# GpSimd's weight sums cut into small pieces and moved in front of the pair sums; two token sums moved behind the last pair's additions

## The chip, the cores and the metric

The kernel runs on one core of one Trainium2 chip. The metric is the device time of one execution in microseconds (us), the median of several runs. Before the change it is 717.16 us (three runs, 717.06 to 717.26).

## The reference

One transformer block over 2048 tokens of width 1024, in bfloat16: a linear attention with 32 heads behind a layer norm, and a gated feed-forward network of inner width 3584.

```python
def reference(A_x, A_wqkv, A_wo, B_x, B_W_gate, B_W_up, B_W_down):
    def _A_ref(x, wqkv, wo):
        ...
        phi = lambda t: jnp.where(t > 0, t + 1, jnp.exp(t)) + 1e-6
        pq, pk = phi(q), phi(k)
        kv = jnp.einsum("bhsd,bhse->bhde", pk, v)
        z = jnp.einsum("bhsd->bhd", pk)
        num = jnp.einsum("bhqd,bhde->bhqe", pq, kv)
        den = jnp.einsum("bhqd,bhd->bhq", pq, z)[..., None] + 1e-6
        o = num / den
        return ... @ wo
    def _B_ref(x, W_gate, W_up, W_down):
        ...
        h = gate * up
        return jnp.einsum("bsf,fd->bsd", h, W_down)
    x = A_x
    h = x + _A_ref(_layernorm(x, axis=-1), A_wqkv, A_wo)
    h2 = h + _B_ref(_layernorm(h, axis=-1), B_W_gate, B_W_up, B_W_down)
    return h2
```

## The kernel before

Nearly all matrix products go by Strassen's scheme with seven products in place of eight (P1 to P7), which needs sums of blocks of the weights and of the tokens beforehand, and additions of the partial results afterwards. TensorE (PE) runs the products; VectorE (DVE), ScalarE (ACT) and GpSimd (POOL) make the sums, the copies between PSUM banks ("forks": a bank's partial sum is copied into a second bank, and both are then accumulated further) and the additions.

The order of work is written out by hand. The program is one list of operations for each engine; every engine runs its own list strictly in order, and an operation waits on semaphores for what it reads and for the last users of what it overwrites. DMAs are issued almost all from SyncE's list (SP), in order as well. A list of hooks says between which products of PE the other engines' operations are put into their lists.

The change lies in the stage of the output projection `@ wo` (about 169 to 226 us of the span) and at its seam with the feed-forward stage. The stage has two parts:

- **Ten direct tiles**, d = 0 to 9, of 128 tokens each: `a4_mm(d)` issues 16 plain matmuls of 512 columns into a pair of banks; between them, at places that the table `at` names, `nd` issues the attention quotient of a later tile: `a2_num` (32 small matmuls on PE, into banks 0 to 3) and `a2_div` (three operations on DVE, L1320, L1323, L1325, and the transposing DMA "T3d" on SP, L641, which fills `oT`). So `nd` at tile d makes the token tile d + 4. For d up to 7, `a4_h(d)` adds the residual (DVE, L1465) into one of three slots of `hsb`, stores that row block by DMA, and makes the statistics of the second layer norm: `mean` and `square` on ACT (L885), each followed by small one-column operations on POOL (L891, L906, L909, and "lnn", L1481). `a4_norm(d - 1)` then normalises the tile before (ACT, L1491) and, up to tile 3, issues its transposing DMA "T5d" into `hnT`; those of 4 to 7 are issued later. Tiles 8 and 9 have their residual put into the banks beforehand by ACT (`a4_pre`, "hx") and are read out by ACT.
- **Three pairs of tiles by Strassen**, `o_group(p0)`, `o_group(p0 + 1)`, `o_group(p0 + 2)`, for the tiles 10/11, 12/13, 14/15. The products come in the order P1, P7, P6, P2, P5, P4, P3, four matmuls each. P7, P6, P5 and P3 read the pair sums So3, So2, So1, So4 (`o_sums`, POOL, L1383); P7, P6, P5 and P4 read weight sums TWo3, TWo2, TWo1, TWo4 (`wo_sums`, POOL, L1366). P6 goes into a bank that the fork "ofk1" (ACT, L850) fills from P1's bank, and P5 into one that "ofk2" fills from P6's. The additions `fin` (DVE, L1422) leave the residual stream of the pair in `hp_home`: tile 11 in the slot of `hsb` that held tile 8. The last addition of a pair and its store wait in `o_pend` until hook 1 of the next.

POOL has three more duties in this stage. TWo3 and TWo1 are made during the query products before it, in eight pieces of 128x512. TWo2 and TWo4 are made behind the tiles 2 to 5, in four pieces of 128x1024 (`tw`). And the weight sums T1 to T4 of the feed-forward stage's first unit (`pool_t`, L1572, eight pieces of 128x512) are spread from tile 6 to the end of the last pair. DVE makes the token sums S1 to S4 of the feed-forward stage (`ss`, L1548, 128x2048 each) in hooks 1, 3, 5 and 7 of the last pair; they need the `hnT` of tiles 0 to 7.

The feed-forward stage begins with unit 0: P1 for two halves (banks 1 and 0), each followed by a fork "fk1" (ACT, L850, into banks 4 and 5), one product P5 with S1, then P2 into banks 1 and 0, and so on; S2, S3 and S4 are read later in the unit, by P6, P7 and P3. On DVE it begins with four sums "xs" (L1628) and three "g1" (L1606).

Of the kernel before, what the change touches and what calls it, by code (L numbers as in the profile page):

```python
# [6 lines left out]
ALU = mybir.AluOpType  # L7
# [125 lines left out]
def bass_sequential_preLN__linear_attn_block__glu_gated_reglu__prompt_kernel(  # L133
# [34 lines left out]
    KH = NDC // 2  # L168
# [8 lines left out]
    TPP = TOK // P  # L177
# [27 lines left out]
    with es:  # L205
# [9 lines left out]
        NXN = 4  # L215
# [76 lines left out]
        xo = RA[:, 12 * D:16 * D].rearrange("p (a b) -> p a b", a=NXN)  # L292
# [79 lines left out]
        s2 = sb("s2", [P, 2, 5], f32)  # L372
# [7 lines left out]
        def bank(b, w=512):  # L380
            return ps[:, b, 0:w]
# [40 lines left out]
        B_bank = bufs("bank", 8)  # L422
# [521 lines left out]
        def run(ops, n):  # L944
            for _ in range(min(n, len(ops))):
                ops.pop(0)()
# [410 lines left out]
        def wo_sums(j, eng, k0, k1, deps=()):  # L1357
            def w(k, h):
                return wo[:, k * KH + k0:k * KH + k1, h * NW:(h + 1) * NW], [B_wo[h]]

            def t(i):
                return TWo(i)[:, k0:k1, :], [B_TWo[i]]

            x, y = {2: lambda: (w(1, 1), w(0, 1)), 0: lambda: (w(0, 1), w(0, 0)), 1: lambda: (w(1, 1), t(0)),
                    3: lambda: (w(1, 0), t(1))}[j]()
            PL.add(eng, lambda e: e.tensor_tensor(out=t(j)[0], in0=x[0], in1=y[0], op=ALU.subtract),  # L1366
                   reads=x[1] + y[1], writes=[B_TWo[j]], deps=deps, name="TWo%d" % (j + 1))
# [15 lines left out]
            PL.add(eng, lambda e: e.tensor_tensor(out=s(i)[0], in0=x[0], in1=y[0], op=op), reads=x[1] + y[1],  # L1383
                   writes=[B_So[z][i]], name="So%d_%d" % (i + 1, p))

        def o_group(p, bks, hooks, fin_eng):
            sa, sb2 = 2 * p, 2 * p + 1
            z = p % 2
            a, f, b, c = bks
            s7, sc, fx = (btmp[:, 1, :], B_bt[1]), (btmp[:, 0, :], B_bt[0]), (Ef[:, z, :], B_Ef[z])  # L1390

            def X(k, t):
                st = 2 * p + t
                return (lambda kk: oT(st)[:, k * KH + kk, :]), [B_oT[st % NOT]]

            def SX(i):
                return (lambda kk: So[:, z, i, kk, :]), [B_So[z][i]]

# [12 lines left out]
            def hook(i):  # L1411
                for f_ in o_pend.pop(i, ()):
                    f_()
                for f_ in hooks.get(i, ()):
                    f_()

            def half(st, h):
                return hp_home[st][:, h * NW:(h + 1) * NW], B_hp[st][h]

            def fin(d, bk, o, nm, eng="dve"):  # L1420
                i = [bank(bk), [B_bank[bk]]] if isinstance(bk, int) else bk
                PL.add(eng, lambda e: e.tensor_tensor(out=d[0], in0=i[0], in1=o[0], op=ALU.add), reads=i[1] + o[1],  # L1422
                       writes=[d[1]], name=nm)
# [24 lines left out]
            fin(half(sb2, 1), [sc[0], [sc[1]]], (fx[0], [fx[1]]), "hp_%d_1" % sb2, fin_eng)  # L1448
            hook(5)
            prod(b, X(1, 1), TW(3), False, "P4")  # L1450
            fin(half(sb2, 0), b, (s7[0], [s7[1]]), "h_%d_0" % sb2)
            store(sb2)
            hook(6)
            prod(c, SX(3), W(1, 1), False, "P3")
            o_pend[1] = [lambda: fin(half(sa, 1), c, res(sa, 1), "h_%d_1" % sa), lambda: store(sa)]
            hook(7)

        o_pend = {}

        def a4_h(st):  # L1460
            xs = x2_slot(st)
            hs = st % NHS
            b = a4_bank.pop(st)
            if st < TPP:
                PL.add("dve", lambda e: e.tensor_tensor(out=hsb[:, hs, :], in0=ps[:, b:b + 2, :],  # L1465
                                                        in1=x2(st).rearrange("p (a c) -> p a c", a=2), op=ALU.add),
                       reads=[B_bank[b], B_bank[b + 1], B_x2[xs]], writes=[B_hs[hs]], name="h_%d" % st)
            dma(sl_hs[hs], ov[st * P:(st + 1) * P, :], hsb[:, hs, :], "st_h_%d" % st, reads=[B_hs[hs]],
                writes=[B_hscr[st]])
            if st + 2 < NDIR:  # L1470
                a4_pre(st + 2)
# [5 lines left out]
            for f_ in act_stats(src, [B_hs[hs]], xo[:, st % NXN, :], B_xo[st % NXN], s2[:, ks, 0:4], B_s2[ks],  # L1477
                                "ln2_%d" % st):
                f_()
            m_, r_, n_ = s2[:, ks, 0:1], s2[:, ks, 2:3], s2[:, ks, 4:5]  # L1480
            PL.add("pool", lambda e: e.tensor_scalar(out=n_, in0=m_, scalar1=r_, scalar2=-1.0, op0=ALU.mult,  # L1481
                                                     op1=ALU.mult),
                   reads=[B_s2[ks][0], B_s2[ks][2]], writes=[B_s2[ks][4]], name="lnn_%d" % st)
# [940 lines left out]
        def sums(p, *what):  # L2424
            return [lambda i=i, e=e: o_sums(p, i, e) for i, e in what]

        def tw(j, k0):
            return lambda: wo_sums(j, "pool", k0, k0 + 2)

        def t5(st):  # L2430
            return lambda: a4_t(st)

        def ldx(st):
            return lambda: load_x2(st)

        def pt():
            run(pool_t, 1)

        p0 = NDIR // 2
        at = {0: {15: [nd]}, 1: {14: [nd]}, 2: {13: [nd]}, 3: {11: [nd]}, 4: {9: [nd]}, 5: {7: [nd]},  # L2440
              6: {5: [nd]}, 7: {3: [nd]}, 8: {1: [nd, t5(4)], 14: [nd, ldx(13), ldx(12)]}, 9: {11: [nd]}}
        aft = {2: [tw(1, 0)], 3: [tw(1, 2)], 4: [tw(3, 0)], 5: [tw(3, 2)], 6: [pt, pt],
               7: sums(p0, (2, "pool"), (0, "pool")), 8: sums(p0, (1, "pool"), (3, "pool")) + [pt]}
        H_PAIRS.sort(key=lambda b: max(bank_last[b], bank_last[b + 1]))
        for d in range(2):
            a4_pre(d)
        for d in range(NDIR):
            a4_mm(d, at.get(d, {}))
            a4_h(d)
            run(late_phi, 1)  # L2450
            if 1 <= d <= TPP:
                a4_norm(d - 1)
            if d < 2:
                load_w_next()
            for f_ in aft.get(d, ()):
                f_()
        o_group(p0, [4, 6, 5, 7], {
            1: [nd, t5(5), t5(6)], 6: [t5(7), ldx(15), ldx(14)],
            4: sums(p0 + 1, (2, "pool"), (0, "pool"), (1, "pool"), (3, "pool"))}, "dve")
        load_w_next()  # L2460
        o_group(p0 + 1, [4, 2, 5, 7], {
            2: sums(p0 + 2, (2, "pool"), (0, "pool"), (1, "pool"), (3, "pool")), 6: [pt]}, "dve")
        load_w_next()
        o_group(p0 + 2, [4, 6, 5, 7], {1: [pt, ss[0]], 2: [pt], 3: [ss[1]], 5: [ss[2]], 7: [ss[3]]}, "dve")
        for f_ in o_pend.pop(1):
            f_()
        run(pool_t, len(pool_t))
        for q in range(NWR):
            load_wraw(q)
        load_w_next()  # L2470
# [179 lines left out]
```

## Time and profile before

| | |
|---|---|
| median of the runs | 717.16 us (717.06 to 717.26) |
| profiled execution, its own time | 717.18 us |
| its span, first to last instruction | 715.5 us |
| PE busy | 703.6 us, 98% of the span |
| DVE busy | 608.7 us, 85% |
| ACT busy | 413.1 us, 58% |
| POOL busy | 144.1 us, 20% |
| granted TensorE clock | 1.00 throughout |

All times below are microseconds from the start of the span. In the timeline view a line has the start, the duration, the engine, the source line, the operation, the tiles written and read, the shape and how many were merged; in square brackets stand the engine's idle time before it and what ended that. A matmul of 512 columns is shown as 0.38 long, but the next one starts 0.216 later (a product of four starts 0.86 after the product before it), so the time that PE really lost at a wait is the distance between the starts less that cadence, some 0.16 more than the idle time shown.

### The profile page before, as it was taken

The numbers are of one execution on the slowest core, as the hardware profiler recorded it, in microseconds if no ns is written. First come the engines' busy times: TensorE is split into PE (matmuls) and PEld (weight loads), VectorE is DVE, ScalarE is ACT, GpSimd is POOL, SyncE is SP. The second block draws the span as 40 slices with busy tenths as digits, with TensorE's granted clock in tenths as the row PEclk, the third lists the DMA queues.
The fourth block names the chain that finished last, engine by engine and source line by source line (L and its number), as shares of the span: only waits on it lengthen the run. The fifth ranks groups of instructions, "written<-read, shape, count | busy, mean of one in ns | idle before, by whom it ended". The sixth has DMA issues, their size and how long they took to land.

```text
span 715.5 us, 13215 instructions
## 1 busy us (share of the span) xinstructions
PE 703.6 (98%) x4984; PEld 392.9 (55%) x5039; DVE 608.7 (85%) x974; ACT 413.1 (58%) x744; POOL 144.1 (20%) x202
## 2 busy tenths in 40 slices
PE   9999999999999999999999999999999999999998
PEld 4444444444443445454544558865555555547887
DVE  7988867899868899999998787788889888988985
ACT  4887666764963777887786401036666667633010
POOL 3321100111797213132312002310000000000331
PEclk9999999999999999999999999999999999999999
DMA  9753345015997899999897999995343534267997
GB/s 301 258 98 81 38 131 165 23 31 97 208 219 203 272 342 296 322 251 294 264 312 225 267 249 318 316 234 161 90 132 112 155 107 131 80 206 250 324 317 186
DMA packets 195104, 144.21 MB, mean 202 GB/s; under 512 B 53984, under 2 KB 172512, under 8 KB 195040
## 3 DMA queue, kind: packets, MB, share of 16 engines
q1 hardware_dynamic: 190048, 138.77, 67.1%
q0 software_dynamic: 4032, 3.67, 3.5%
q8 instruction: 40, 0.66, 0.4%
q10 hardware_dynamic: 960, 0.92, 0.4%
q14 instruction: 24, 0.20, 0.1%
HBM read 98.76 MB, written 32.51 MB: 183 GB/s over the span
## 4 chain that ended last, share of the span: by engine, by line
PE 91%; DVE 5%; issue 2%; ACT 1%; DMA 1%; DVEq 0%; ACTq 0%
PE ps L845 91%; DVE RC L1548 1%; DMA RAB<-RXH 1%; DVE RO L1572 1%; DVE RAB L1422 0%; DVE RAB L1706 0%; ACT RXH L885 0%; DMA RE<-in_A_x_dram 0%; DVE RW L781 0%; ACT ps L850 0%; ACT RX L850 0%; DVE RWG L1093 0%; PE ps L1006 0%; DVE ps L1706 0%; DVE RE L1967 0%
## 5 line engine op out<-in xcount | busy, mean ns | idle before, releaser
L850 ACT ACTIVATE ps<-ps 128x512 f32<-128x512 f32 (+1 forms) x263 | 133.1, 517 | 180.4 <-PE ps L845 127.6
L845 PE MATMUL ps<-RC,RO 128*128 128x512 f16 x616 | 147.0, 369 | 0.0
L845 PEld LDWEIGHTS ps<-RC,RO 128*128 128x128 f16 x616 | 60.1, 98 | 53.1 <-ACT ps L850 1.2
L850 ACT ACTIVATE RE<-ps 128x512 f32<-128x512 f32 (+3 forms) x106 | 63.8, 627 | 31.7 <-PE ps L845 17.6
L845 PE MATMUL ps<-RC,RWG 128*128 128x512 f16 x320 | 80.8, 379 | 0.0
L845 PE MATMUL ps<-RH,RWG 128*128 128x512 bf16 (+1 forms) x347 | 77.6, 348 | 1.4 <-ACT ps L850 1.4
L1976 POOL DMA_DIRECT2D out_dram<-RX x20 | 17.9, 1258 | 271.5 <-DVE RX L1967 218.4
L845 PE MATMUL ps<-RH,RO 128*128 128x512 bf16 (+1 forms) x228 | 59.2, 379 | 1.5
L1706 DVE TENSOR_TENSOR RE<-ps,RE 128x1024 bf16<-128x1024 f32 (+1 forms) x42 | 44.0, 1047 | 18.2 <-PE ps L845 18.1
L845 PE MATMUL ps<-RW,RAB 128*128 128x256 f16 (+3 forms) x370 | 55.6, 303 | 0.2
L845 PEld LDWEIGHTS ps<-RH,RWG 128*128 128x128 bf16 x348 | 33.9, 98 | 36.9 <-ACT ps L850 2.0
L845 PE MATMUL ps<-RAB 128*128 128x512 bf16 (+3 forms) x248 | 52.6, 349 | 1.1 <-ACT ps L850 0.8
L845 PEld LDWEIGHTS ps<-RC,RWG 128*128 128x128 bf16 (+1 forms) x320 | 30.0, 98 | 34.4 <-ACT ps L850 5.8
L845 PEld LDWEIGHTS ps<-RW,RAB 128*128 128x128 f16 (+1 forms) x374 | 36.3, 98 | 16.2 <-ACT RX L850 1.1
L1967 DVE TENSOR_TENSOR RE<-ps,RE 128x512 f32<-128x512 f32 x44 | 30.2, 686 | 14.4 <-PE ps L845 11.8
L1718 ACT ACTIVATE RAB<-RAB 128x1024 bf16<-128x1024 bf16 x28 | 29.5, 1054 | 19.0 <-DVE RAB L1706 19.0
L1706 DVE TENSOR_TENSOR RAB<-ps,RE 128x1024 bf16<-128x1024 f32 x28 | 34.2, 1222 | 7.3 <-PE ps L845 6.9
L1706 DVE TENSOR_TENSOR RAB<-RAB,RE 128x1024 bf16<-128x1024 bf16 x56 | 37.2, 685 | 3.2 <-ACT RE L850 2.8
L1572 DVE TENSOR_TENSOR RO<-RWG 128x1024 f16<-128x1024 bf16 x54 | 39.4, 729 | 0.0
L850 ACT ACTIVATE RX<-ps 128x512 f32<-128x512 f32 (+1 forms) x40 | 23.5, 597 | 25.9 <-PE ps L845 22.7
L1572 DVE TENSOR_TENSOR RO<-RWG,RO 128x1024 f16<-128x1024 bf16 x54 | 38.2, 708 | 0.0
L845 PEld LDWEIGHTS ps<-RH,RO 128*128 128x128 f16 (+1 forms) x256 | 24.4, 98 | 24.6 <-ACT RX L850 1.5
(214 smaller groups left out, 1298.4 us busy)
## 6 DMA issues: line engine op xcount, KB each, us to landing
RWG<-in_B_W_gate_dram SPq DMA_DIRECT2D x28, 512.0 KB, 6.2
RWG<-in_B_W_up_dram SPq DMA_DIRECT2D x28, 512.0 KB, 5.0
RW<-l_scr SPq DMA_DIRECT2D x20, 448.0 KB, 5.6
RW<-in_B_W_down_dram SPq DMA_DIRECT2D x14, 512.0 KB, 5.8
t_scr<-RW SPq DMA_DIRECT2D x14, 512.0 KB, 4.4
l_scr<-RX SPq DMA_DIRECT2D x7, 1024.0 KB, 7.8
RE<-l_scr SPq DMA_DIRECT2D x15, 448.0 KB, 5.2
RW<-t_scr SPq DMA_DIRECT2D x13, 448.0 KB, 5.6
```

Source lines behind the costliest of these rows:

```text
L845: lambda e: e.matmul(out_ap, lhsT, rhs, start=start, stop=stop, skip_group_check=skip),
L850: PL.add("act", lambda e: e.activation(out=dst, in_=src, func=func), reads=reads, writes=writes, name=name)
L1548: PL.add("dve", lambda e: e.tensor_tensor(out=Ssum[:, i], in0=in0, in1=in1, op=op), reads=reads, writes=[B_S[i]], name="S%d" % (i + 1))
L1572: PL.add(eng, lambda e: e.tensor_tensor(out=tb(j, u), in0=f0(u), in1=f1(u), op=ALU.subtract), reads=[B_w[i + x] for x in r] + ([B_T[k + x] ...
L1706: PL.add("dve", lambda e: e.tensor_tensor(out=dst, in0=in0, in1=in1, op=op), reads=reads, writes=writes, name=name)
L1718: PL.add("act", lambda e: e.activation(out=d, in_=d, func=ACTF.Relu), reads=[], writes=db, name=name)
L1967: PL.add(eng, lambda e: e.tensor_tensor(out=dst, in0=in0, in1=in1, op=op), reads=reads, writes=writes, name=name)
L1976: PL.add("pool", lambda e: e.dma_start(dst, src, accum_op=ALU.add), reads=[bsrc], writes=[B_hscr[st]], slot=sl, name="acc_%d_%d" % (st, dh))
```

## The change

In words, by engine:

- **POOL, weight sums.** TWo2 and TWo4 are made in eight pieces of 128x512 in place of four of 128x1024. They and the eight pieces of `pool_t` form one queue of sixteen: two are issued in front of tile 0, then two in each of the tiles 0 to 6, one behind the store of the tile (`mid`) and one between the operations for `mean` and those for `square` (`mid2`). The pieces in front of tile 0 and the first ones of tiles 0 and 1 also wait for DVE's last operation issued so far. After tile 6 the queue is empty.
- **POOL, pair sums.** Those of the first pair, which stood behind the statistics of tiles 7 (So3, So1) and 8 (So2, So4), stand in tile 7: So3 in `mid`, So1 in `mid2`, So2 and So4 behind tile 7's statistics. Those of the other pairs keep their hooks.
- **ACT.** `a4_norm(7)` moves from tile 8 to hook 1 of the first pair, behind its fork "ofk1".
- **PE, DVE.** Two of the `nd` are issued a little earlier: that of tile 7 by one matmul, that of tile 9 by two. The leftover phi steps of the last query product (`late_phi`) are issued before `a4_pre` and the statistics, which leaves DVE's order as it is.
- **SP.** The loads of the residual tiles 13 and 12 move from tile 8 to tile 9, behind the store of tile 8 and the T3d of tile 14.
- **DVE.** The addition of the two SBUF operands (`hp_..._1`) is a `scalar_tensor_tensor` (times 1.0, plus) in place of a `tensor_tensor`. S3 and S4 move from hooks 5 and 7 of the last pair behind its last addition and store.

```diff
-    def fin(d, bk, o, nm, eng="dve"):
-        i = [bank(bk), [B_bank[bk]]] if isinstance(bk, int) else bk
-        PL.add(eng, lambda e: e.tensor_tensor(out=d[0], in0=i[0], in1=o[0], op=ALU.add), reads=i[1] + o[1],
-               writes=[d[1]], name=nm)
+    def fin(d, bk, o, nm):
+        PL.add("dve", lambda e: e.tensor_tensor(out=d[0], in0=bank(bk), in1=o[0], op=ALU.add),
+               reads=[B_bank[bk]] + o[1], writes=[d[1]], name=nm)
...
-    fin(half(sb2, 1), [sc[0], [sc[1]]], (fx[0], [fx[1]]), "hp_%d_1" % sb2, fin_eng)
+    d21, db21 = half(sb2, 1)
+    PL.add("dve", lambda e: e.scalar_tensor_tensor(out=d21, in0=sc[0], scalar=1.0, in1=fx[0], op0=ALU.mult,
+                                                   op1=ALU.add),
+           reads=[sc[1], fx[1]], writes=[db21], name="hp_%d_1" % sb2)
...
-def a4_h(st):
+def a4_h(st, mid, mid2):
...
+    mid()
     if st + 2 < NDIR:
         a4_pre(st + 2)
...
-    for f_ in act_stats(...):
-        f_()
+    mean, square = act_stats(...)
+    mean()
+    mid2()
+    square()
...
 def tw(j, k0):
-    return lambda: wo_sums(j, "pool", k0, k0 + 2)
+    return lambda deps=(): wo_sums(j, "pool", k0, k0 + 1, deps)
+pool_q = [tw(j, k0) for j in (1, 3) for k0 in range(KH)] + pool_t
+def pq():
+    if pool_q:
+        pool_q.pop(0)()
+def last_dve():
+    return PL.prog["dve"][-1:]
...
-      6: {5: [nd]}, 7: {3: [nd]}, 8: {1: [nd, t5(4)], 14: [nd, ldx(13), ldx(12)]}, 9: {11: [nd]}}
-aft = {2: [tw(1, 0)], 3: [tw(1, 2)], 4: [tw(3, 0)], 5: [tw(3, 2)], 6: [pt, pt],
-       7: sums(p0, (2, "pool"), (0, "pool")), 8: sums(p0, (1, "pool"), (3, "pool")) + [pt]}
+      6: {5: [nd]}, 7: {2: [nd]}, 8: {1: [nd, t5(4)], 14: [nd]}, 9: {9: [nd, ldx(13), ldx(12)]}}
+so = sums(p0, (2, "pool"), (0, "pool"), (1, "pool"), (3, "pool"))
...
+pool_q.pop(0)(last_dve())
+pq()
 for d in range(NDIR):
     a4_mm(d, at.get(d, {}))
-    a4_h(d)
-    run(late_phi, 1)
-    if 1 <= d <= TPP:
+    def mid(d=d):
+        run(late_phi, 1)
+        if d < 2:
+            pool_q.pop(0)(last_dve())
+        elif d < TPP - 1:
+            pq()
+        elif d < TPP:
+            so[0]()
+    a4_h(d, mid, pq if d < TPP - 1 else so[1])
+    if 1 <= d < TPP:
         a4_norm(d - 1)
     if d < 2:
         load_w_next()
-    for f_ in aft.get(d, ()):
-        f_()
+    if d == TPP - 1:
+        so[2]()
+        so[3]()
 o_group(p0, [4, 6, 5, 7], {
-    1: [nd, t5(5), t5(6)], 6: [t5(7), ldx(15), ldx(14)],
-    4: sums(p0 + 1, (2, "pool"), (0, "pool"), (1, "pool"), (3, "pool"))}, "dve")
+    1: [nd, t5(5), lambda: a4_norm(TPP - 1)], 2: [t5(6)],
+    4: sums(p0 + 1, (2, "pool"), (0, "pool"), (1, "pool"), (3, "pool")), 6: [t5(7), ldx(15), ldx(14)]})
 load_w_next()
 o_group(p0 + 1, [4, 2, 5, 7], {
-    2: sums(p0 + 2, (2, "pool"), (0, "pool"), (1, "pool"), (3, "pool")), 6: [pt]}, "dve")
+    2: sums(p0 + 2, (2, "pool"), (0, "pool"), (1, "pool"), (3, "pool"))})
 load_w_next()
-o_group(p0 + 2, [4, 6, 5, 7], {1: [pt, ss[0]], 2: [pt], 3: [ss[1]], 5: [ss[2]], 7: [ss[3]]}, "dve")
-for f_ in o_pend.pop(1):
+o_group(p0 + 2, [4, 6, 5, 7], {1: [ss[0]], 3: [ss[1]]})
+for f_ in o_pend.pop(1) + ss[2:]:
     f_()
-run(pool_t, len(pool_t))
```

More of the change, by code (lines that the diff above doesn't have):

```diff
@@ L1384, in o_sums, with o_group @@
                    writes=[B_So[z][i]], name="So%d_%d" % (i + 1, p))
-        def o_group(p, bks, hooks, fin_eng):
+        def o_group(p, bks, hooks):
             sa, sb2 = 2 * p, 2 * p + 1
@@ L1476, in a4_h @@
             src = hsb[:, hs, :]
-            for f_ in act_stats(src, [B_hs[hs]], xo[:, st % NXN, :], B_xo[st % NXN], s2[:, ks, 0:4], B_s2[ks],
-                                "ln2_%d" % st):
-                f_()
+            mean, square = act_stats(src, [B_hs[hs]], xo[:, st % NXN, :], B_xo[st % NXN], s2[:, ks, 0:4], B_s2[ks],
+                                     "ln2_%d" % st)
+            mean()
+            mid2()
+            square()
             m_, r_, n_ = s2[:, ks, 0:1], s2[:, ks, 2:3], s2[:, ks, 4:5]
@@ L2434, in ldx @@
             return lambda: load_x2(st)
-        def pt():
-            run(pool_t, 1)
         p0 = NDIR // 2
         at = {0: {15: [nd]}, 1: {14: [nd]}, 2: {13: [nd]}, 3: {11: [nd]}, 4: {9: [nd]}, 5: {7: [nd]},
-              6: {5: [nd]}, 7: {3: [nd]}, 8: {1: [nd, t5(4)], 14: [nd, ldx(13), ldx(12)]}, 9: {11: [nd]}}
-        aft = {2: [tw(1, 0)], 3: [tw(1, 2)], 4: [tw(3, 0)], 5: [tw(3, 2)], 6: [pt, pt],
-               7: sums(p0, (2, "pool"), (0, "pool")), 8: sums(p0, (1, "pool"), (3, "pool")) + [pt]}
+              6: {5: [nd]}, 7: {2: [nd]}, 8: {1: [nd, t5(4)], 14: [nd]}, 9: {9: [nd, ldx(13), ldx(12)]}}
+        so = sums(p0, (2, "pool"), (0, "pool"), (1, "pool"), (3, "pool"))
         H_PAIRS.sort(key=lambda b: max(bank_last[b], bank_last[b + 1]))
@@ L2454, in bass_sequential_preLN__linear_attn_block__glu_gated_reglu__prompt_kernel @@
                 load_w_next()
[L2455 to L2456 removed]
+            if d == TPP - 1:
+                so[2]()
+                so[3]()
         o_group(p0, [4, 6, 5, 7], {
[L2458 to L2459 removed]
+            1: [nd, t5(5), lambda: a4_norm(TPP - 1)], 2: [t5(6)],
+            4: sums(p0 + 1, (2, "pool"), (0, "pool"), (1, "pool"), (3, "pool")), 6: [t5(7), ldx(15), ldx(14)]})
         load_w_next()
         o_group(p0 + 1, [4, 2, 5, 7], {
[L2462 removed]
+            2: sums(p0 + 2, (2, "pool"), (0, "pool"), (1, "pool"), (3, "pool"))})
         load_w_next()
[L2464 to L2465 removed]
+        o_group(p0 + 2, [4, 6, 5, 7], {1: [ss[0]], 3: [ss[1]]})
+        for f_ in o_pend.pop(1) + ss[2:]:
             f_()
[L2467 removed]
+        assert not pool_q
         for q in range(NWR):
```

## The prediction

> **What bounds the kernel now.** I read the page first, then PE's waits, then the timeline from 160 to 240 us.
>
> ```profile
> span 715.5 us, 13215 instructions
> PE 703.6 (98%) x4984; PEld 392.9 (55%) x5039; DVE 608.7 (85%) x974; ACT 413.1 (58%) x744; POOL 144.1 (20%) x202
> PE ps L845 <- ACT ps L850: 2.5, 3, 1.4
> PE ps L845 <- POOL RXH L618: 1.4, 1, 1.4
> ```
>
> PE is busy all but about 12 us, and of the 2.5 us that it waits for ACT's forks 2.2 lie in two waits of this stage. So the change can only win what PE loses here. The places are in the timeline (all engines but those named left out):
>
> ```profile
> 206.64 0.37 PE L845 MATMUL ps<-kvz,RAB 32*128 32x33 bf16 x32 [0.28 <-DVE RE L1325]
> 212.44 1.20 DVE L1422 TENSOR_TENSOR RXH<-RX 128x512 bf16<-128x512 f32 x1 [1.37 <-DMA out_dram<-RXH]
> 214.28 0.58 ACT L850 ACTIVATE ps<-ps 128x512 f32<-128x512 f32 x1 [3.03 <-DVE RXH L1422]
> 214.91 1.04 PE L845 MATMUL ps<-RAB 128*128 128x512 f16 x4 [0.84 <-ACT ps L850]
> 227.10 2.17 DVE L1548 TENSOR_TENSOR RC<-RH 128x2048 f16<-128x2048 bf16 x1
> 229.19 0.68 DVE L1422 TENSOR_TENSOR RAB<-ps,RX 128x512 bf16<-128x512 f32 x1
> 229.79 1.21 DVE L1548 TENSOR_TENSOR RC<-RH,RC 128x2048 f16<-128x2048 bf16 x1
> 229.90 0.58 ACT L850 ACTIVATE ps<-ps 128x512 f32<-128x512 f32 x1 [2.67 <-DVE RAB L1422]
> 230.54 1.04 PE L845 MATMUL ps<-RH,RWG 128*128 128x512 bf16 x4 [1.39 <-ACT ps L850]
> ```
>
> Three losses are seen. At 206.64 PE waits for the quotient of tile 14 (0.28 idle, 0.35 by the starts: 205.33 to 206.64 is 1.31, less 0.86 for four matmuls and 0.1 for the turn). At 214.91 it waits for ofk1 of the second pair, which waits for tile 11's addition, behind an addition that sat 1.37 until the store of tile 8 had landed (starts 213.04 to 214.91, less 0.86: 1.0). At 230.54 it waits for the second fk1, which waits for an addition of the last pair that stood in DVE's list behind S3 (starts 228.12 to 230.54, less 0.86: 1.55). Together 2.9 us.
>
> The fourth place is no wait yet:
>
> ```profile
> 199.58 1.29 SPq L641 DMA_TRANSPOSE RX<-RE x1
> 202.01 0.31 POOL L891 TENSOR_SCALAR s<-s 128x1 f32<-128x1 f32 x1
> 203.58 0.27 POOL L1481 TENSOR_SCALAR s<-s 128x1 f32<-128x1 f32 x1
> 203.80 2.27 POOL L1383 TENSOR_TENSOR RAB<-RX 128x512 f16<-128x512 bf16 x2
> 206.15 1.15 POOL L1383 TENSOR_TENSOR RAB<-RAB,RX 128x512 f16<-128x512 f16 x1
> 207.82 1.03 PE L845 MATMUL ps<-RAB 128*128 128x512 f16 x4
> ```
>
> So2 of the first pair ends at 207.30, 0.5 us before the P6 that reads it (207.82). So3 needs tile 11's transpose, issued by SP at 199.58; its landing stands in the trace at 203.49.
>
> **S3 and S4 behind the additions.** Before, POOL's T pieces ran beside S1 to S3, which took 2.10, 2.09 and 2.17 us; S4, with POOL done, took 1.21. Now POOL has no T left there. The last pair's additions on DVE then follow only S1 and S2: S1 from 220.4 to 221.6, two additions, S2 to about 223.9, and the four left at 0.6 to 0.7 each, so that the one that releases fk1 ends near 226.0 (each waits only for its product, the latest ending at 225.7) in place of 229.87. fk1 can follow PE's P1 at 227.5, and P2 needs it at 229.0: cover 0.9 us. The wait goes: **-1.55**. Late next are S3 and S4 themselves, 226.5 to 228.9 in place of 231.0, then the four xs (0.42 each) and the first g1, ready near 231.0; the product that reads them comes at 233.46 - 1.55 = 231.9. It waited some 0.1 us before; I count nothing.
>
> **The pieces in the direct tiles.** In tiles 2 to 5 one 2.13 us piece and the statistics give POOL a period of 3.77 (starts 184.61, 188.38, 192.15). Two pieces of 1.16 in its place make 3.96; a tile takes PE 3.43 (187.20 less 183.77). So POOL falls behind PE by 0.5 a tile. It starts tile 1's share behind the last leftover phi step (ends 178.00), at 178.1, and gets to So3 after six tiles at 178.1 + 6 x 3.96 = 201.9. The data come at 203.49, so the lag costs nothing here: cover 1.6 us. On ACT, tile 4's norm follows POOL's lnn at 193.9 in place of 193.28; behind it stands hx of tile 8, at 195.1 in place of 194.92, needed by PE at 197.2. The later norms were at 198.10 and 202.40, POOL's results are there at 197.9 and 201.9. T1's first pieces want the weights landed at 179.9 and 186.5. Cost nothing; if a piece took 0.13 more, the cover would be gone.
>
> **The pair sums of the first pair.** This is the step that costs. POOL's list now reads So3, the small _v, So1, the three small ones, So2. So3 can start at 203.49 + 0.16 (a later pair sum starts 0.16 after its landing) = 203.65. Then 1.25 (piece and gap), 0.26 (_v), 1.25, 0.27, 0.66, 0.22 (the small ones by their starts in tile 7: 202.64, 202.91, 203.58, 203.80) and 1.16 for So2: it ends at 208.7, and P6 starts at 208.8 in place of 207.82. **+0.98**, and the 0.35 won at 206.64 (tile 14's nd is two matmuls, 0.43, earlier) is swallowed in it. Bounds: So3 at the group's median landing (3.6 after issue, 203.2) gives 208.5; with the landing unchanged but the small operations free it would be 207.4 and the cost nothing.
>
> **SP, tile 8's store.** SP's list is never empty from 182 to 219, so order is time there: the store of tile 8 moves ahead of two loads, from 208.52 to about 207.45, and lands near 211.3 (3.9 later). The loads, issued near 209.5 and landing 3.6 later at 213.1 and 213.6, are read at 214.8 and 216.9: free. Tile 14's transpose comes 1 us earlier, read only by the last pair. The addition behind the store then waits for osc instead, which is 0.98 later with P6 (212.2), and may be stretched by POOL's So2 of the second pair (1.20, as in the row; alone 0.69, the row at 218.50). Tile 11's addition ends at 213.5 to 214.1. By then ofk1 is bound by P1 of that pair (213.16 + 0.65 + 0.38 = 214.2), so the wait of 1.0 goes: **-1.0**. Added to P6's +0.98, PE stands at P6 of the second pair at 214.9, where it stood before. From there to the seam all inputs come as before (tile 15's transpose, last to be read, still issued near 211.2).
>
> As for the `scalar_tensor_tensor`: the trace has this form with both inputs in SBUF, POOL idle, at 0.69, the same as the `tensor_tensor`. Bounds 0.69 and 1.20; I take up to 1.20, and both leave ofk1 bound by P1. A rule bears on it. The Trainium skill, "SBUF — State Buffer", section "Who interferes with whom", says a DVE instruction with two SBUF inputs and a GpSimd instruction reading SBUF exclude one another, the second waiting out the whole first. The rows half agree: S3 took 2.17 for 1.21, but POOL's pieces beside it took 3.69 for two in place of 2.27, so both sides pay. By the rule the new form gains nothing; if it escaped the lock, 0.5 us earlier there, hidden by P1. The sum is the same.
>
> **norm of tile 7** (1.23 on ACT, behind ofk1) waits for POOL's lnn at 207.6 and ends at 208.9; the fork behind it, ofk2, waits for P6 to end at 209.8. Cost nothing, cover 0.9. Its T5d is issued behind the store of tile 11, as before.
>
> **Sum.** +0.98 - 1.0 - 1.55 = -1.57, say -1.6, from the profiled execution's 717.18 (span 715.5 and 1.7 around it; 0.02 above the median): **715.6 us**, 0.22% faster. About 0.2% (1.43 us) is what a measurement here can tell from no change, so the forecast stands at that bound.
>
> **Rivals.**
> A. The small operations hide and So2 is in time. For it: POOL overlaps the start of an independent operation with the end of the one before (starts 1.11 apart for 1.15 long). Against: the chain is six operations on one engine. Then the 1.0 and 0.35 are won as well: 717.2 - 2.9 = 714.3.
> B. So2 is later than I count, because tile 11's transpose lands later or So1 or So2 is stretched, by 0.5 to 1.2. It passes one for one to PE: 716.1 to 716.8. For it: transposes in this stage took 3.0 to 6.1 to land.
> C. The fork still waits at the seam, or S3/S4 or xs are late and the same wait comes one product later: 717.2. Against: 0.9 us of cover.
> D. Slower: POOL's pieces run at the contended rate. The T pieces beside S2 and S3 took 1.63 and 1.85. Fourteen such in the tiles lag 14 x 0.5 to 0.7 = 7 to 10 us, less the cover of 1.6: PE waits 5 to 8 us at P6 and ends at 720.6 to 724. It decides from about 1.4 a piece (0.13 for the cover, 0.11 for the 1.55 gained). Against: DVE's work in the direct tiles has one SBUF input, and POOL's 2.13 pieces ran there unstretched.
>
> **How the numbers follow.** Forecast 0.55 (own range 715.1 to 716.1), A 0.13, B 0.14, C 0.10, D 0.08. The range goes down to A's 714.3 and up to C's 717.2, taken as 717.3; outside it lie D and the lower half of A, 0.15. Faster by over 0.2% (below 715.73): all of A and two thirds of the forecast case, 0.5; within: the rest of the forecast, B and most of C, 0.38; slower: D, and 0.04 of C (the wait returns later and longer), 0.12.
>
> **What would show it.** Right: no PE wait near 229 to 230 and S1 to S4 at 1.21; P6 of the first pair waiting about 1.3 for POOL's L1383 near 208; none at 214.9; POOL idle about 1.6 for a DMA near 202 to 203.5. Wrong if POOL has no idle there (D), P6 doesn't wait (A), or a wait for ACT or DVE stands in the first unit of the feed-forward stage (C).

## The result, and the profile after

The changed kernel takes **715.91 us** (median of 20 runs, 714.77 to 717.01), the kernel before in the same comparison 717.28 us (20 runs). The ratio is **0.9974, 95% interval 0.9967 to 0.9982**. The forecast was 715.6, in a range of 714.3 to 717.3. The ratios follow the means, and so they feel the few runs that are 1 to 4 us longer than the rest (five of before's twenty here, 718.46 to 720.12; four of e7's twelve below, 718.46 to 720.02; one of e5's, 921 us, counts in its median alone): the gain here is 1.37 us by the medians and 1.85 by the means. Each ratio below is to runs of the kernel before that were taken along with it, whose medians lie between 716.98 and 717.37.

The profiled execution has a time of 715.36 us. First the span on the page of the changed kernel, then PE's waits (engine, line, what was waited for: us in total, times, longest):

```profile
span 713.6 us, 13274 instructions
```

```profile
PE ps L845 <- POOL RAB L1383: 1.1, 1, 1.1
PE ps L845 <- ACT ps L850: 0.3, 1, 0.3
```

ACT's forks, which PE waited for three times and 2.5 us in all, are down to one wait of 0.3, which lies outside this stage. In their place stands one wait of 1.1 for a pair sum of POOL.

The timeline of the changed kernel at the places that the prediction named:

```profile
203.16 1.16 POOL L1383 TENSOR_TENSOR RAB<-RX 128x512 f16<-128x512 bf16 x1 [2.74 <-DMA RX<-RE]
206.95 1.15 POOL L1383 TENSOR_TENSOR RAB<-RAB,RX 128x512 f16<-128x512 f16 x1
208.25 1.02 PE L845 MATMUL ps<-RAB 128*128 128x512 f16 x4 [1.05 <-POOL RAB L1383]
211.63 1.15 POOL L1383 TENSOR_TENSOR RAB<-RAB,RE 128x512 f16<-128x512 f16 x1
211.77 1.56 DVE L1448 SCALAR_TENSOR_TENSOR RXH<-RX 128x512 bf16<-128x512 f32 x1 [0.84 <-ACT RX L850]
213.47 1.03 PE L845 MATMUL ps<-RXH,RAB 128*128 128x512 f16 x4
213.97 0.58 ACT L850 ACTIVATE ps<-ps 128x512 f32<-128x512 f32 x1 [2.29 <-DVE RXH L1421]
214.60 1.04 PE L845 MATMUL ps<-RAB 128*128 128x512 f16 x4
222.44 1.21 DVE L1553 TENSOR_TENSOR RC<-RC,RH 128x2048 f16<-128x2048 f16 x1
225.01 0.68 DVE L1421 TENSOR_TENSOR RAB<-ps,RX 128x512 bf16<-128x512 f32 x1
227.22 0.58 ACT L850 ACTIVATE ps<-ps 128x512 f32<-128x512 f32 x1 [0.28 <-PE ps L845]
227.82 1.89 PE L845 MATMUL ps<-RH,RWG 128*128 128x512 bf16 x8
```

The reader sees four things. POOL reached So3 2.74 us ahead of its data (203.16), so the small pieces in the tiles did no harm. So2 ended at 208.10, and P6 of the first pair (208.25) waited 1.05 for it. P6 of the second pair (214.60) shows no wait, though by the starts it is 0.27 later than the cadence of 0.86 (213.47 to 214.60). And at the seam S2 takes 1.21 (as do S1, S3 and S4, to 0.01), the addition that releases the second fk1 ends at 225.69 in place of 229.87, and PE goes through both halves of P2 (eight matmuls from 227.82) without a gap.

**A measure for the stage.** In every execution the head of the kernel takes a little more or less, whatever is changed here: the first quotient product of the stage (the 32 small matmuls of tile 4) starts between 151.56 and 152.74 us. So I count from that product to the first product of unit 0 that reads xs and g1. This stretch is 81.43 us before (152.03 to 233.46) and 79.90 after (151.59 to 231.49). What lies behind it, to PE's end, takes 479.20 to 479.35 us in all fourteen profiled executions. So what the change and the experiments do to a profiled execution is, but for 0.15, inside the stretch; it is read from one execution of each kernel. The table gives it with the times; the experiments are described below.

| kernel | stretch, us | median, us (runs) | ratio to before, 95% interval |
|---|---|---|---|
| before | 81.43 | 717.28 (20) | |
| after | 79.90 | 715.91 (20) | 0.9974 (0.9967 to 0.9982) |
| e1: S3, S4 moved, alone | 80.56 | 716.34 (11) | 0.9988 (0.9979 to 0.9997) |
| e4: order of nd and loads, alone | 80.75 | 716.91 (11) | 0.9992 (0.9981 to 1.0003) |
| e13: e1 and e4 together | 79.97 | 716.31 (12) | 0.9989 (0.9980 to 0.9997) |
| e2: after, S3 and S4 back | 80.06 | 715.33 (7) | 0.9975 (0.9964 to 0.9985) |
| e5: after, plain addition | 79.88 | 715.99 (12) | 0.9974 (0.9964 to 0.9985) |
| e7: after, one piece more ahead of So2 | 80.26 | 716.51 (12) | 0.9994 (0.9980 to 1.0007) |
| e8: after, two pieces more | 80.33 | 715.87 (12) | 0.9977 (0.9963 to 0.9991) |
| e9: after, six pieces more | 84.23 | 720.21 (10) | 1.0034 (1.0021 to 1.0048) |
| e3: after, statistics ahead of the pair sums | 78.56 | 714.33 (5) | 0.9959 (0.9947 to 0.9972) |
| e11: the same as e3 | 78.81 | 714.30 (5) | 0.9954 (0.9941 to 0.9967) |
| e10: e3 with the loads as before | 78.84 | 715.19 (9) | 0.9969 (0.9958 to 0.9979) |
| e12: before again | 81.12 | 717.81 (1) | |

### The profile page after: what moved, and what is told of

It reads as the page before. It is cut to its first block, busy times and chain, and to the rows that moved or that the text cites. A ratio compares the mean times of both kernels' runs of the same rounds, so it can differ in the third digit from the quotient of the medians.

```text
span 713.6 us, 13274 instructions
## 1 busy us (share of the span) xinstructions
PE 707.4 (99%) x5039; PEld 392.3 (55%) x5039; DVE 606.2 (85%) x974; ACT 413.4 (58%) x744; POOL 142.3 (20%) x206
## 4 chain that ended last, share of the span: by engine, by line
PE 93%; DVE 3%; DMA 1%; issue 1%; ACT 1%; POOL 1%; SPq 0%; DVEq 0%; POOLq 0%
PE ps L845 92%; DMA RAB<-RXH 1%; DVE RC L1068 0%; POOL RAB L1383 0%; DMA RX<-RE 0%; DVE RW L1068 0%; DVE RWG L1093 0%; DMA RE<-in_A_x_dram 0%; ACT RXH L885 0%; DVE RE L1972 0%; DVE st L859 0%; DVE RX L1184 0%; DVE RE L1325 0%; DVE RXH L1467 0%; ACT ps L850 0%
## 5 line engine op out<-in xcount | busy, mean ns | idle before, releaser
L845 PE MATMUL ps<-RH,RO 128*128 128x512 bf16 (+1 forms) x256 | 65.3, 379 | 0.0
```

What stands on the lines that cost most here:

```text
L845: lambda e: e.matmul(out_ap, lhsT, rhs, start=start, stop=stop, skip_group_check=skip),
```

## The experiments

### e1: the move of S3 and S4 alone

The kernel before, with the two sums behind the last additions; POOL's list stays as it was.

```diff
-o_group(p0 + 2, [4, 6, 5, 7], {1: [pt, ss[0]], 2: [pt], 3: [ss[1]], 5: [ss[2]], 7: [ss[3]]}, "dve")
-for f_ in o_pend.pop(1):
+o_group(p0 + 2, [4, 6, 5, 7], {1: [pt, ss[0]], 2: [pt], 3: [ss[1]]}, "dve")
+for f_ in o_pend.pop(1) + ss[2:]:
```

> The kernel before with one thing changed: S3 and S4 stand behind the last pair's additions. My theory says the wait of 1.55 us at the seam goes by this alone, although S1 and S2 stay stretched by POOL's T pieces: the addition that releases the second fk1 follows the one that ends at 227.2, ends near 227.8, and the fork has until 229.0. So 1.55 us less than before, ratio 0.9978; the wait of 1.0 us at P6 of the second pair and that of 0.35 us for tile 14's quotient stay. The rival, that only an empty POOL list frees the seam, says no change (ratio 1.000), with the fork still waiting.

Measured: 716.34 us, ratio 0.9988 (0.9979 to 0.9997), about half of what I expected of the move. The fork's wait is gone, but PE waits at a later product. Timeline of this kernel:

```profile
219.18 1.15 POOL L1383 TENSOR_TENSOR RAB<-RE,RAB 128x512 f16<-128x512 bf16 x1
219.45 1.96 DVE L1548 TENSOR_TENSOR RC<-RH 128x2048 f16<-128x2048 bf16 x1 [0.23 <-DMA RH<-RAB]
220.29 2.14 POOL L1572 TENSOR_TENSOR RO<-RWG,RO 128x512 f16<-128x512 bf16 x1
222.53 2.09 DVE L1548 TENSOR_TENSOR RC<-RC,RH 128x2048 f16<-128x2048 f16 x1
227.31 2.08 DVE L1548 TENSOR_TENSOR RC<-RH 128x2048 f16<-128x2048 bf16 x1
232.38 0.39 PE L845 MATMUL ps<-RX,RAB 128*128 128x256 f16 x2 [1.59 <-DVE RAB L1606]
```

S1, S2 and S3 still take 1.96 to 2.09 beside POOL's pieces. DVE's list is as long as before, so what is taken out from in front of the fork stands in front of the four xs and the three g1, and the product that reads those waits 1.59. That is the form of rival C. The move alone shifts the wait; it doesn't remove it. In the kernel before, too, the first g1 ended at 233.40 and the product that reads it started at 233.46, so a second wait stood behind the fork's, ready to take its place. Most of the 0.87 us by which this stretch is shorter than before was won elsewhere: P6 of the second pair has no wait in this execution (it starts at 213.74, 0.90 behind P7), though nothing ahead of it was edited, and S1 starts 67.63 us into the stretch in place of 68.28. From S1's start to the end of the first g1 DVE takes 12.87 us in place of 13.09.

### e2: everything but that move

The changed kernel, with S3 and S4 back in hooks 5 and 7.

```diff
-o_group(p0 + 2, [4, 6, 5, 7], {1: [ss[0]], 3: [ss[1]]})
-for f_ in o_pend.pop(1) + ss[2:]:
+o_group(p0 + 2, [4, 6, 5, 7], {1: [ss[0]], 3: [ss[1]], 5: [ss[2]], 7: [ss[3]]})
+for f_ in o_pend.pop(1):
```

> The changed kernel with S3 and S4 back in hooks 5 and 7 of the last pair. Theory: with POOL's list empty S3 takes 1.21 us and the addition behind it ends near 226.9 of the changed kernel's time, before the fork can start at 227.2, so the time is that of the changed kernel (ratio to before 0.997 to 0.998). The move and the empty POOL are then two sufficient causes for the same wait. Rival: the move itself is what wins at the seam, and 1.0 to 1.55 us come back (ratio 0.999 to 1.000).

Measured: 715.33 us, 0.9975 (0.9964 to 0.9985), the same as the full change. The timeline of this kernel, with the addition that releases the second fk1 standing behind S3 as before:

```profile
225.94 1.21 DVE L1553 TENSOR_TENSOR RC<-RH 128x2048 f16<-128x2048 bf16 x1
227.08 0.68 DVE L1421 TENSOR_TENSOR RAB<-ps,RX 128x512 bf16<-128x512 f32 x1
227.85 0.58 ACT L850 ACTIVATE ps<-ps 128x512 f32<-128x512 f32 x1 [0.28 <-DVE RAB L1421]
228.45 1.89 PE L845 MATMUL ps<-RH,RWG 128*128 128x512 bf16 x8
```

With S1 to S3 at 1.21, the fork is ready at 228.43. P2's eight matmuls start at 228.45; the four that need the second fork are the last four, which follow at 229.31. So there is 0.9 us to spare, without the move. What removes the wait at the seam is POOL's empty list, not DVE's new order; e1 and e2 together show that the first is needed and that the second, beside it, is not.

### e4 and e13: the orders without the moved pieces

e4 is the kernel before with the changed table for `nd` and the two loads. e13 is e4 with e1's edit on top: the reordering of the quotients, of the two loads and of DVE's sums, with POOL's list as before.

```diff
-      6: {5: [nd]}, 7: {3: [nd]}, 8: {1: [nd, t5(4)], 14: [nd, ldx(13), ldx(12)]}, 9: {11: [nd]}}
+      6: {5: [nd]}, 7: {2: [nd]}, 8: {1: [nd, t5(4)], 14: [nd]}, 9: {9: [nd, ldx(13), ldx(12)]}}
```

> The kernel before with only the places of the quotients (tiles 7 and 9) and of the loads of residual tiles 13 and 12 changed as in the change; POOL's list, S3 and S4 as before. Theory: So2 is in time there (207.3 against P6 at 207.5), the wait for tile 14's quotient goes (0.35 us), and tile 8's store lands about 1 us earlier, which takes 0.8 to 1.0 us from the second pair's wait: 1.2 us less than before, ratio 0.9983; the seam's wait stays. Rival: the store's landing isn't what counts, the addition behind it stays late, and only 0.35 us is won (ratio 0.9995).

> The kernel before with both orders of the change (quotients and loads, and S3 and S4 behind the last additions), but POOL's list as before: the T pieces still run beside S1, S2 and S3. Theory: DVE's stretched list is what bounds the seam, so PE gets there up to 1.3 us earlier and waits for it, at the first g1, by 1.6 to 2.9 us; 0.5 to 1.2 us less than before, ratio 0.9985 to 0.9993. Rival: the parts add up without the pieces, and it comes to the 714.3 us of the best kernel, ratio 0.996.

Measured: e4 716.91 us, 0.9992 (0.9981 to 1.0003), not told from no change, where 1.2 us less was expected; e13 716.31 us, 0.9989 (0.9980 to 0.9997). In e4 PE waits neither for the quotient of tile 14 nor for the second pair's ofk1, but the waits of the seam have grown, to 1.56 at the fork and 0.29 at g1. Timeline of e13:

```profile
223.69 2.09 DVE L1548 TENSOR_TENSOR RC<-RC,RH 128x2048 f16<-128x2048 f16 x1
228.46 1.21 DVE L1548 TENSOR_TENSOR RC<-RH 128x2048 f16<-128x2048 bf16 x1
232.66 0.39 PE L845 MATMUL ps<-RX,RAB 128*128 128x256 f16 x2 [1.07 <-DVE RAB L1606]
```

Here POOL is done before S3, which takes 1.21, but S1 (2.08) and S2 (2.09) are still 0.87 and 0.88 too long, and the wait at g1 is 1.07, less than the 1.6 to 2.9 expected. It hangs on a tenth of a us whether the moved S3 still meets POOL's last piece: in e1 that piece runs from 227.16 to 228.31 and S3, from 227.31, takes 2.08; here POOL's list ends at 228.35 and S3 starts at 228.46. From S1's start to the end of the first g1 DVE takes 12.12 us here, where it took 12.87 in e1 and 13.09 before. So without the pieces the move can win from 0.2 us to 1.0, the latter where it carries S3 past POOL's list. How much the moved pieces add to the orders is seen differently by the two measures: after is 1.1 us (ratios) or 0.4 (medians) faster than e13, but its stretch only 0.07 shorter. The trace shows why there is little: after has no wait at g1, but 1.05 at P6 of the first pair in its place.

### e12: the kernel before, a second profile

No edit. This run asks how much of the waits shown before belongs to that one execution.

> The kernel before, unchanged, for a second profile. Theory: the wait at the seam is there again at 1.3 to 1.6 us in the fork or in the first sums behind it, since DVE's list sets it; the wait at the second pair's P6 (0.84 idle in the first profile) depends on when one store lands and can be anything from 0 to 1. Rival: both stand as in the first profile.

Measured: 717.81 us (one run), stretch 81.12. Timeline:

```profile
217.90 1.15 POOL L1383 TENSOR_TENSOR RAB<-RAB,RE 128x512 f16<-128x512 f16 x1
218.24 1.37 DVE L1422 TENSOR_TENSOR RAB<-RX 128x512 bf16<-128x512 f32 x1 [0.91 <-ACT RX L850]
230.94 1.04 PE L845 MATMUL ps<-RH,RWG 128*128 128x512 bf16 x4 [2.02 <-ACT ps L850]
```

The second pair's wait of 1.0 is absent from this execution (P6 at 214.65 has none), without any change. It hangs on when one store lands: the addition that has to wait for it starts 59.3 us into the stretch here (212.04 less 152.74), and started at 60.4 there (212.44 less 152.03). In e1, with the same order of SP's list, the wait was absent too: of these three executions only the first has it. But the time isn't won: the wait at the seam is 2.02 in place of 1.39, above the 1.3 to 1.6 expected. Between the two, DVE's addition at 218.24 falls into a pair sum of POOL's and takes 1.37; in the other execution it took 0.69. So the waits in a row of this stage don't add up: the last one, which DVE's list sets, takes in most of what is won ahead of it.

### e3 and e11: the statistics of tile 7 ahead of the pair sums

The changed kernel, with the four pair sums of the first pair behind tile 7's eight small operations on POOL. This takes the small ones out of the chain from the data of So3 to the end of So2. So3 and So1 stood behind these statistics in the kernel before, too: e3 takes that part of the change back and keeps the rest.

```diff
-        elif d < TPP:
-            so[0]()
-    a4_h(d, mid, pq if d < TPP - 1 else so[1])
+    a4_h(d, mid, pq if d < TPP - 1 else lambda: None)
...
-        so[2]()
-        so[3]()
+        for f_ in so:
+            f_()
```

> The changed kernel with the four pair sums of the first pair behind tile 7's statistics on POOL, in place of between them. POOL sat idle 2.7 us there for tile 11's transpose, so the small operations fit into that. Theory: So2 ends near 206.7, P6 of the first pair no longer waits for POOL (1.05 us idle in the changed kernel), and the second pair's fork is bound by its own P1 again: 1.0 us less than the changed kernel, about 714.9 us where that has 715.9, ratio to before 0.996. Rival: the wait only moves on to the second pair's fork, behind the addition of two SBUF operands, and less than 0.3 us is won.

> The kernel with tile 7's statistics ahead of the first pair's sums once more, for more runs and a second profile. Theory: 714.3 to 715.0 us, ratio to before 0.996, no wait of PE above 0.2 us in the stage or in the first unit behind it. Rival: the first runs were lucky ones and it lies with the changed kernel at 0.9974.

Measured: 714.33 us, 0.9959 (0.9947 to 0.9972), and 714.30 us, 0.9954 (0.9941 to 0.9967). **This version beats both kernels**, the changed one by 1.6 us by the medians, and by 1.1 to 1.3 in the stretch, where 1.0 was expected. Timeline of e3:

```profile
203.59 0.27 POOL L1486 TENSOR_SCALAR s<-s 128x1 f32<-128x1 f32 x1
203.81 2.27 POOL L1383 TENSOR_TENSOR RAB<-RX 128x512 f16<-128x512 bf16 x2
206.16 1.15 POOL L1383 TENSOR_TENSOR RAB<-RAB,RX 128x512 f16<-128x512 f16 x1
207.48 1.03 PE L845 MATMUL ps<-RAB 128*128 128x512 f16 x4
211.00 0.69 DVE L1448 SCALAR_TENSOR_TENSOR RXH<-RX 128x512 bf16<-128x512 f32 x1 [0.26 <-ACT RX L850]
211.06 1.65 POOL L1383 TENSOR_TENSOR RAB<-RAB,RE 128x512 f16<-128x512 f16 x1
```

The small operations now fill the 2.74 us in which POOL had waited for a DMA. So3 starts when they are done, So2 ends at 207.31, and P6 goes at the cadence. In e3 nothing in this stage makes PE wait for more than 0.16 us; in e11 P6 of the second pair waits 0.23.

### e5: the addition as a plain tensor_tensor

The changed kernel, with the old form of the addition of the two SBUF operands.

```diff
-PL.add("dve", lambda e: e.scalar_tensor_tensor(out=d21, in0=sc[0], scalar=1.0, in1=fx[0], op0=ALU.mult,
-                                               op1=ALU.add),
+PL.add("dve", lambda e: e.tensor_tensor(out=d21, in0=sc[0], in1=fx[0], op=ALU.add),
```

> The changed kernel with the addition of two SBUF operands as a tensor_tensor again. In the changed kernel the scalar_tensor_tensor of the first pair took 1.56 us beside a pair sum of POOL, and the fork behind it started at 213.97 where its own product would have let it start near 213.7. Theory: the new form escapes nothing; the old one takes about 1.2 beside POOL, the fork starts up to 0.25 us earlier and the time is that of the changed kernel or up to 0.25 us less (ratio to before 0.997 to 0.998). Rival: the new form was the faster one, and the old one takes over 1.6 and costs 0.2 us or more.

Measured: 715.99 us, 0.9974 (0.9964 to 0.9985). The plain addition took 1.57 us, not the 1.2 expected, where it began 0.13 behind a piece of POOL's; the other form took 1.56 in the same position. The form does nothing here.

### e7, e8, e9: how much cover POOL has

The changed kernel, with a piece of TWo2 made again: one ahead of So2 (e7), one each in tiles 3 and 4 (e8), one each in tiles 1 to 6 (e9). Nothing is left out; the extra work writes the same values once more.

```diff
@@ e7
+        tw(1, 0)()
         so[2]()
@@ e8, e9
-    a4_h(d, mid, pq if d < TPP - 1 else so[1])
+    def mid2(d=d):
+        pq()
+        if d in (3, 4):      # e9: (1, 2, 3, 4, 5, 6)
+            tw(1, 0)()
+    a4_h(d, mid, mid2 if d < TPP - 1 else so[1])
```

> The changed kernel with one more POOL piece of 128x512 (a weight sum made a second time, same values) in front of So2 of the first pair, about 1.2 us. Theory: P6 is bound by So2 there, so it starts 1.2 us later, the wait for POOL grows from 1.05 to about 2.3, and the end is 1.2 us later: about 717.1 where the changed kernel has 715.9, ratio to before 0.999. Rival: the stage behind has slack of its own (the second pair's store and transposes come late anyway) and swallows half of it or more.

> The changed kernel with one more POOL piece of 128x512 (made a second time, same values) in each of the direct tiles 3 and 4: 2.4 to 2.5 us more on POOL. In the changed kernel POOL sat idle 2.74 us in front of So3. Theory: the cover holds it; POOL's idle time shrinks to 0.2 to 0.4 and the time is that of the changed kernel (ratio to before 0.997 to 0.998). Rival: POOL's lag reaches PE by ACT (norms, and the residual put into the banks of tile 8) before the cover is used up, and 0.5 us or more is lost.

> The same with one more piece in each of the tiles 1 to 6: 7.2 to 7.5 us more on POOL, 4.5 to 4.8 beyond the 2.74 of cover. Theory: POOL becomes the bound of the direct tiles; PE waits 4.5 to 5 us more, at P6 of the first pair or, by ACT's norms, at the products whose banks ACT must empty, and the time is about 720.5 (ratio to before 1.004 to 1.005). Rival: less than half of it, since other waits are hidden behind it.

Measured: e7 716.51 us, 0.9994 (0.9980 to 1.0007), which is 0.6 (medians) to 1.4 (ratios) above the changed kernel. The 1.4 rests on the four long runs; the other eight have a median of 716.37, 0.46 above, nearer to the rival of this run (half or more is swallowed) than to the expected 1.2. Its profile shows only 1.22 of wait at P6, and a stretch 0.35 longer: in that execution So3 could start at 202.23, some 0.9 earlier than after, because tile 11's transpose landed earlier. So the mechanism of rival B stands with its sign; that a later So2 passes one for one to PE is not shown.

e8 715.87 us: 2.3 us more on POOL in the tiles cost nothing that the times tell, though the stretch is 0.43 longer than after. POOL still waits 0.87 for So3's data; the profile has one new wait of PE, 0.46 at 197.81, for the residual that ACT puts into the banks of tile 8. e9 720.21 us, 1.0034 (1.0021 to 1.0048): 4.3 us above the changed kernel. Timeline of e9:

```profile
198.45 1.24 ACT L1496 ACTIVATE RAB<-RXH,s 128x1024 bf16<-128x1024 bf16 x1 [1.45 <-POOL s L1486]
199.60 1.01 ACT L850 ACTIVATE ps<-RE 128x1024 f32<-128x1024 bf16 x1
200.66 0.39 PE L845 MATMUL ps<-RW,RE 128*128 128x512 bf16 x1 [2.92 <-ACT ps L850]
```

Most of it is not lost where rival D had it, at P6 (0.5 there), but two tiles earlier: ACT's norm of tile 4 waits for POOL's lnn, the residual hx of tile 8 stands behind the norm in ACT's list, and PE waits 2.92 for hx at the first matmul of tile 8. Behind that wait the granted clock is 0.50 from 201.97 to 205.38, and matmuls of 512 columns start 0.43 apart in place of 0.216: from the quotient product in tile 8 to the next one it takes 4.90 us (200.98 to 205.88), where it took 3.22 in the changed kernel (197.06 to 200.28). So some 1.7 of the 4.3 us are lost to the clock, which the expectation had not counted; that its 720.5 us fits so well is in part luck. The path through ACT is one that the prediction had costed (at nothing, for the change), and it shows first in e8. So POOL's lateness reaches PE through ACT before it reaches it through the pair sums, and the cover ends somewhat below e8's 2.3 us.

### e10: the loads back in tile 8

e3, with the loads of the residual tiles 13 and 12 ahead of tile 8's store again.

```diff
-      6: {5: [nd]}, 7: {2: [nd]}, 8: {1: [nd, t5(4)], 14: [nd]}, 9: {9: [nd, ldx(13), ldx(12)]}}
+      6: {5: [nd]}, 7: {2: [nd]}, 8: {1: [nd, t5(4)], 14: [nd, ldx(13), ldx(12)]}, 9: {9: [nd]}}
```

> The kernel with tile 7's statistics ahead of the first pair's sums, but with the loads of residual tiles 13 and 12 back in tile 8, ahead of tile 8's store. The prediction gave this order of SP's list 1.0 us. Theory after the first runs: the store then lands about 1 us later, near 210.4, and the addition that overwrites its source starts near 211.0 when ACT's osc is done, so most of the time nothing waits for it and the time is that of the other kernel within 0.3 us (ratio to before 0.996). Rival, the prediction's own step: the order is worth up to 1.0 us (ratio 0.997 to 0.9975), with the addition waiting for the store and the second pair's P6 behind it.

Measured: 715.19 us, 0.9969 (0.9958 to 0.9979), against 714.30, 0.9954 (0.9941 to 0.9967), of e11 on the same chip. In the profile DVE's addition waits 0.58 for the store and P6 of the second pair 0.26, but e11 has 0.23 at that P6 too, and the stretches are 78.84 and 78.81. In e10 the addition waits for the store and in e11 for POOL's piece (it takes 1.69 there); in both it ends 60.7 us into the stretch, in e3, where it started ahead of POOL's piece, at 59.7. By the medians the order of the loads is worth 0.9 us, and eight of e10's nine runs are longer than the longest of e11's five (714.47); by these two executions it is worth nothing. The times differ, but that the order makes the difference is not shown.

## Why the prediction was right

Direction and size came as forecast: -1.6 forecast against the profiled execution, -1.82 measured for it, of which 0.44 is a faster head that the change has no part in, and 0.14 went the other way behind the stage. In the stretch it is -1.53. That this comes within 0.04 of the forecast is in part luck: against e12's stretch of 81.12 the change wins 1.22. Term by term, each by PE's starts counted from the first quotient product:

| step | forecast | measured |
|---|---|---|
| first pair, P6 (55.79 to 56.66) | +0.98 | +0.87 |
| second pair, P6 (62.88 to 63.01, less the line above) | -1.0 | -0.74 |
| seam (81.43 to 79.90, less the lines above) | -1.55 | -1.66 |
| sum | -1.57 | -1.53 |

**The pair sums of the first pair.** Right in mechanism and size. The chain from So3's start to So2's end took 4.94 us (203.16 to 208.10) where the forecast's seven operations, from 203.65 to 208.7, gave 5.05 (rival A counts them as six). The wait of 0.35 for the quotient of tile 14 went and was swallowed, as written: that product started at 205.85 and P6 was late all the same. e3 and e11 show the counterpart: with the small operations in the idle time the time is 714.3, rival A's price to the tenth of a us, though A had got there by another way.

**The pieces in the direct tiles.** Free, as costed, with more cover than counted: POOL's period is 3.79 (starts 181.45, 185.24, 189.03, 192.82), not 3.96, so that cutting a piece in two cost 0.02 a tile and not 0.19. Over six tiles that makes 1.0 us more of idle time in front of So3 (2.74 in place of 1.6). e8 shows that 2.3 us more are nearly free, e9 that 7 are not.

**The second pair.** The wait went, but 0.27 of delay stayed. The step that failed is "up to 1.20, and both leave ofk1 bound by P1": the addition took 1.56, which makes the next additions late, and ofk1 starts at 213.97, when the one at 213.26 has ended, 0.24 later than P1 would have allowed (0.26 behind P7's start, as e3's ofk1). And by e12 the term as a whole belongs to one execution as much as to the kernel: where the store happens to land early, as in e12 and in e1, the 1.0 isn't there to be won; in e12 the seam has taken most of it.

**The seam.** Right in size, since the working counted POOL's T pieces as gone and S1 and S2 at 1.21. But the name over the step, "S3 and S4 behind the additions", gives the gain to the wrong edit, and so did my expectation of e1. The gain is that DVE's sums are no longer stretched; once POOL's list is empty the move buys nothing that the times tell (e2). What rival C described, the same wait one product later, is what the move does without the pieces (e1, and in part e13).

**Norm of tile 7, SP's order, xs and g1.** No wait shows at any of them, as costed. The store of tile 8 landed 2.6 us after its issue (206.62 to 209.18), where 3.9 was counted.

The chances: the case forecast came, and the time of 715.91 lies inside its own range of 715.1 to 716.1. The profile's marks were met: no wait near 229 to 230, S1 to S4 at 1.21 and 1.22, P6 of the first pair waiting for POOL (1.05, about 1.3 was written), none listed at P6 of the second, POOL idle for a DMA (2.74, about 1.6 was written).

## What to carry to other kernels

Put small independent operations into the idle time before an operation that waits for a DMA, and nothing between that operation and the one that the critical engine waits for: here that order alone is worth 1.6 us by the medians and 1.1 to 1.3 in the stretch, nearly as much as the whole change. When a wait ends at an engine whose list is too long, shorten the list; a new order of it mostly moves the wait to the next reader (e1), unless it also takes work out from beside the other engine's (e13). And don't add up waits that follow one another: see whether the last of them is set by a list that has no slack, for it will take back what is won ahead of it.

## What the runs showed of the hardware that was not expected

DVE and POOL take turns, exactly. In thirteen of the profiled executions, between 206 and 232 us (e9's three cases, some 4 us later, agree), I set each DVE addition or token sum with both inputs in SBUF beside the piece of POOL that was running when it started, and the other way round. In 27 cases a 128x512 addition (0.69 alone) ended 0.54 to 0.55 us after POOL's piece had ended; in one more the two started together, and DVE went first, and in two the addition started in the last 0.1 of the piece and took its own 0.69. In 15 cases a 128x2048 token sum (1.21 alone) ended 1.08 after the piece. In 40 cases a piece of POOL's (1.15 alone) ended 1.01 to 1.02 after DVE's operation. Each is the operation's own time less 0.13 to 0.14, counted from the other's end. So the one that starts second is held until the first is done, and the duration in a profile is that wait plus its own work. An addition with one input in PSUM is not held: 136 of them that started beside a piece of POOL's, in all fourteen executions, took 0.67 to 0.69.

The rows shown above can be followed with it. In the changed kernel POOL's sum at 211.63 ends at 212.78 and the addition at 213.33; in e3 the addition starts 0.06 before POOL's sum, takes its 0.69, and POOL pays with 1.65. In e1 POOL's piece ends at 220.33, S1 1.08 later at 221.41, and POOL's next 1.01 later at 222.43. The prediction read its rows, S3 at 2.17 and POOL's two pieces at 3.69, as a rate that both sides share, and said that they only half agree with the Trainium skill ("SBUF — State Buffer", section "Who interferes with whom": an exclusive lock, held for the whole instruction, and the order of issue decides who is blocked). They agree with it wholly: where both lists are full the engines alternate, and each waits for the other in turn. It also gives the bound that the prediction lacked: an addition beside a 128x512 piece can take up to 1.15 + 0.55 = 1.70, and the longest seen is 1.69, in e11.

A long wait may cost PE more than itself. In e9's profile the granted clock fell to 0.50 for 3.41 us behind a wait of 2.92; behind the waits of 2.02 in e12 and of 1.59 in e1 it stayed at 1.00. Eight of e9's ten runs, the profiled one among them, have a granted clock of 0.998 over the span. No run varies the length of the wait alone, so that the wait is the cause is not shown.
